# A gated mix of a Fourier layer and sliding-window attention: the order of the first loads, the start of a clearing, and three steps moved by a block or two

## The chip, the cores and the metric

One core of one Trainium2 chip. The metric is the device time of one execution in microseconds (us). The core has five engines that run side by side: TensorE (PE; its weight loads are PEld), VectorE (DVE), ScalarE (ACT), GpSimd (POOL) and SyncE (SP), which here issues nearly all transfers. 16 DMA engines carry them.

## The reference

x is 2048 rows of 512 (float32). The reference computes

```python
a, b = x @ dft_hid_re.T, x @ dft_hid_im.T
A = dft_seq_re @ a - dft_seq_im @ b
q, k, v = heads(x @ wqkv)              # 32 heads of 16
p = softmax(q k^T / 4, where 0 <= i - j < 256)
B = (p v, heads side by side) @ wo
g = sigmoid((x * gate_w).sum(-1))
out = g * A + (1 - g) * B
```

## The kernel before

**Products in two parts.** A float32 operand is split into a high part (a cast) and a low part (the value less the high part). A product is three matmuls, high x high, high x low and low x high, summed in PSUM (TERMS, L248). ScalarE, VectorE or GpSimd makes the high part; mostly VectorE makes the low one. `split` (L78) does both: its cast is L80 (ScalarE) or L82, its subtraction L85.

**The head (L147 to L164).** x comes transposed, in 4 slices of 128 input channels (dk) for each quarter `ss` of 512 rows. The first weights, `wqk[0]`, are 1024 columns: 256 (128 KB) for each dk. A slice of x for one `ss` is 128x512, 256 KB. ScalarE's queue issues two of the four slices of x (L155), SP's queue the other two and the four parts of the weights (`ld`, L55/L56). Then, for each dk in turn, ScalarE casts the weights (L162), x is split (for dk 0 both steps on VectorE, else the cast on ScalarE), and VectorE makes the weights' low part (L164). Inside this block the order of ScalarE, VectorE and SP is that of the code. TensorE first runs eight matmuls on zeros (`warm`, L593). `qk_first` (L263, matmuls L269) then makes the first quarter of q and k of head group 0: for each dk, three terms of two matmuls (q and k). `v_proj` (matmuls L304) follows; its weights `wv` are the next loads.

**Clearing (L198 to L219).** The tiles `pads` and `ring` hold q and k of one group in 96 of 128 partitions; 96 to 127 must be zero or hold the row maxima. GpSimd clears them: one `affine_select` into a pad (L203), whose condition never holds, so that every value is the fill 0, and which reads a part of the first x only to be ordered behind it; then eight memsets of 32x2048 (L200), each issued behind the last.

**Attention** runs over n = 4 groups x 32 blocks of 64 queries, 4 pairs of heads p in each. `s_pair` (L357) makes scores against 320 keys (L367); VectorE finds the row extreme (L369), ScalarE exponentiates and sums (L372). Every 8 blocks `ml_split`, `ml_turn` and `ml_rows` turn the extremes and the inverse sums and store them in DRAM (`m_scr`, `l_scr`). LAG = 19 blocks later `t_pair` (L436) makes the scores again, transposed, with keys on partitions, for block k = n - 19 (L449); ScalarE exponentiates (L450), GpSimd masks (L454, L458), and `pv` (L461, matmuls L475) multiplies by v for several blocks in one visit. When 8 blocks of a group are summed, `o_out` (L491) multiplies the sum by the inverse sums (L496) and stores it. `l_load` (L485) loads these inverse sums into one of five `ev` buffers, which also serve the partial results of the Fourier part.

**The Fourier part** is a generator, `dense` (L595). The loop (L1021) takes a few of its matmuls between the attention's (`fill`), so TensorE's order is written out by the code. The sequence products (L529) take pieces of `cr` and `ci`, 128x1024, loaded by SP into two `raw` buffers and split (L588); each piece feeds 24 matmuls. Partial sums go to DRAM (`r_scr`) and back.

**The output projection** (`wo_begin`, L911, matmuls L922) takes seven products for four blocks of a 2x2 split. What it needs first is made ahead of attention's end by the table BEFORE_END (L1007): `first_load` (attention outputs), `first_sums` (L876 to L879, sums on VectorE), `split_a(0)` and four `first_split`. A key (k, p) says after which block and pair a step is issued.

Outside the head a scheduler places the instructions of ScalarE, VectorE, GpSimd and SP; `behind` (L68) holds a step behind the last marked instruction of an engine.

Of the kernel before, what the change touches and what calls it, by code (L numbers as in the profile page):

```python
# [14 lines left out]
P = 128  # L15
S = 2048
D = 512
DK = D // P
NG = 4
NP = 4  # L20
# [12 lines left out]
def fnet_window_mix(ctx: ExitStack, tc: tile.TileContext, xT, x, wqk, wv, wr, wi, cr, ci, wo, gw, out):  # L33
    nc = tc.nc
# [20 lines left out]
    def ld(dst, src):  # L55
        mark("sp", nc.sync.dma_start(dst, src))  # L56

    def f(ap):
        return ap.bitcast(F32)
# [4 lines left out]
    def mark(e, ins):  # L64
        last[e] = ins.ins

    @contextmanager
    def behind(*engines):  # L68
        with ExitStack() as es:
            for e in engines:  # L70
                if e in last:
                    es.enter_context(tc.issue_after(last[e]))
            yield
# [4 lines left out]
    def split(hi, lo, raw, act=False):  # L78
        if act:
            nc.scalar.copy(hi, raw)  # L80
        else:
            cast = (nc.gpsimd if act is None else nc.vector).tensor_copy(hi, raw)  # L82
            if act is None:
                mark("pool", cast)
        return nc.vector.tensor_sub(lo, raw, f(hi))  # L85
# [43 lines left out]
    XT = {}  # L129
    XRAW = {}  # L130
# [7 lines left out]
    def split_x(ss, dks, act=False):  # L138
        for dk in dks:
            XT[dk, ss] = big.tile([P, 2, 512], F32R, name="big")  # L140
            mark("dve", split(XT[dk, ss][:, 0], XT[dk, ss][:, 1], XRAW.pop((dk, ss)), act))


    def pt_raw():
        return at.tile([P, NP, WIN], F32, name="pt", bufs=4).rearrange("p a b -> p (a b)")[:, :1024]

    with tc.manual_schedule(engines={mybir.EngineType.Activation, mybir.EngineType.DVE, mybir.EngineType.SP}):  # L147
        wraw, *xraw = [pt_raw() for _ in range(3)]
        wq0 = [st.tile([P, 1024], F32R, name=h) for h in ("hi", "lo")]
        zero = ev.tile([P, 512], F32R, name="ev")  # L150
        nc.vector.memset(f(zero[:]), 0.0)
        for dk in (0, 2, 1, 3):
            XRAW[dk, 0] = xraw[dk // 2][:, HALVES[dk % 2]]
            if dk % 2 == 0:
                nc.scalar.dma_start(XRAW[dk, 0], xT[0, dk])  # L155
        for dk in range(DK):
            ld(wraw[:, dk * 256:dk * 256 + 256], wqk[0][:, dk * 256:dk * 256 + 256])
            if dk % 2 == 0:
                ld(XRAW[dk + 1, 0], xT[0, dk + 1])
        for dk in range(DK):  # L160
            c = slice(dk * 256, dk * 256 + 256)
            mark("act", nc.scalar.copy(wq0[0][:, c], wraw[:, c]))  # L162
            split_x(0, (dk,), dk > 0)
            mark("dve", nc.vector.tensor_sub(wq0[1][:, c], wraw[:, c], f(wq0[0][:, c])))  # L164
# [3 lines left out]
    pads = [[const.tile([P, NP, P], F32R, name=f"pad{i}_{b}") for b in range(NPAD)] for i in range(2)]  # L168
# [4 lines left out]
    for h in (0, 64):  # L173
        m = mask[h:h + 64, :]
# [23 lines left out]
    def clear_rows(i, ss):  # L198
        with behind("pool"):
            mark("pool", nc.gpsimd.memset(f(ring[i][96:128, :, ss * 512:(ss + 1) * 512]), 0.0))  # L200

    first_hi = f(XT[0, 0][96:128, 0]).rearrange("r (p c) -> r p c", p=NP)
    mark("pool", nc.gpsimd.affine_select(pads[0][0][96:128], first_hi, pattern=[[0, NP], [0, P]],  # L203
                                         compare_op=OP.is_gt, fill=0.0, base=0, channel_multiplier=0))
    for ss in range(4):
        for i in (1, 0):
# [219 lines left out]
    def v_spread(n):  # L426
        if n >= NG * NB:
            return
        raw = VR.pop(n)
        v2 = vpad[n // 4 % 2]  # L430
        for h in range(2):
            nc.gpsimd.tensor_scalar(v2[:, :, :, 16 * h:16 * h + 16], raw.rearrange("r j (p d) -> r j p d", d=16),  # L432
                                    side[:, h:h + 1], None, op0=OP.mult)
        V2[n // 4] = v2
# [358 lines left out]
    def spots(i, n, c0):  # L793
        if c0 + 512 > S:
            return flat(i)[:, c0:c0 + n * S].rearrange("r (p s) -> r p s", s=S)[:, :, :512]
        return ring[i][:, :n, c0:c0 + 512]
# [3 lines left out]
    def os_spot(m, b):  # L800
        if m < 3:
            return spot(0, m, COL[b])
        if b and m == 6:
            return spot(0, 3, COL[0])
        return spot(1, m - 3, COL[b])

    def halves(t):
        return (t[:, :256], t[:, 256:]) if len(t.shape) == 2 else (t[:, :, :256], t[:, :, 256:])
# [7 lines left out]
    def wo_fetch(c):  # L816
        RAW[c] = [const.tile([P, 512], F32, name="tw", tag=f"pad0_{j}") for j in range(2)]
        for j in range(2):
            ld(RAW[c][j], wo[j][:, HALVES[c]])
# [4 lines left out]
    def wo_diffs(c):  # L824
        b11, b12, b21, b22 = (q for t in RAW[c] for q in quarters(t, 2))
        t1, t3, t2, t4 = spare()
        for t, x, y in ((t1, b12, b11), (t3, b22, b12), (t2, b22, t1), (t4, b21, t2)):
            nc.vector.tensor_sub(t, x, y)
        DIFF[c] = b11, b21, b22, t4, t1, t2, t3

    def fin_split(c, m):
        split(fin(m, 0, c), fin(m, 1, c), DIFF[c][m])
# [60 lines left out]
    def split_a(i):  # L893
        a, b = O[i][1]
        split(*halves(spots(0, 2, COL[i % 2])), a.rearrange("p (m t) -> p m t", m=2), True)
        split(*halves(os_spot(2, i % 2)), b[:, 256:], True)

    def first_split(m):
        split(*halves(os_spot(m, 0)), EX[0][m - 3], True)
# [69 lines left out]
    def ring_ahead(n):  # L969
        nonlocal loaded  # L970
        while loaded < 16:
            g, ss = divmod(loaded, 4)
            if n >= 32 * g + 8 * ss:
                need(("qk", g, ss))
            if ("qk", g, ss) not in have or n - LAG < 32 * (g - 1) + 8 * ss + 9:
                break
            with behind(*(("sp",) if g == 0 else ())):
                ring_load(g, ss)
            loaded += 1
# [10 lines left out]
    N = NG * NB  # L990
# [9 lines left out]
    def v_next(n):  # L1000
        if n < N:
            for c in range(2):
                need(("v", n % NB // 2 + c))
            with behind(*(("sp",) if n < 8 else ())):
                v_load(n)

    BEFORE_END = {(121, 3): first_load, (123, 0): first_sums, (123, 2): lambda: split_a(0)}  # L1007
    for c, k in enumerate((113, 118)):
        BEFORE_END[(110, 116)[c], 2] = lambda c=c: wo_fetch(c)
        BEFORE_END[k - 1, 1 + 2 * c] = lambda c=c: wo_diffs(c)  # L1010
        for j, m in enumerate((0, 1, 2, 4, 6, 5, 3)):
            BEFORE_END[k + j // 2, j % 2 * 2] = lambda c=c, m=m: fin_split(c, m)
    for j, m in enumerate((3, 5, 4, 6)):
        BEFORE_END[124 + j // 2, j % 2 * 2] = lambda m=m: first_split(m)

    def ahead_of_end(k, p):
        if (k, p) in BEFORE_END:
            with behind("pad1", "sp"):
                BEFORE_END[k, p]()

    for n in range(N + LAG + 1):  # L1021
        k = n - LAG
        if k == 0:
            masks.append(n)
        ring_ahead(n + 1)
        if k in (-1, 4):
            v_spread(0 if k < 0 else 4)
        if k in (-4, -1, 4):
            v_next({-4: 0, -1: 4, 4: 8}[k])
        if n == 0:  # L1030
            make_pad(0, 0)
        for p in range(NP):
            if n < N:
                s_pair(n, p)
            fill(n)
            visit = p == 0 and (k - summed >= (6 if more else 4) or k == N)
            if 0 <= k < N and not visit:
                t_pair(k, p)
            if p == 0:
                make_pad(0, n + 1)  # L1040
                if k >= -1:
                    make_pad(1, k + 1)
            fill(n)
            if visit:
                for j in range(summed, k):
                    pv(j)
                summed = k
                if k < N:
                    t_pair(k, p)
            ahead_of_end(k, p)  # L1050
            for at_n, at_p, do in TURN if n > 12 else FIRST:
                u, j = divmod(n - at_n, 8)
                if p == at_p and j == 0 and 0 <= u < 16:
                    do(u)
            if p == 3 and k % 8 == 6 and 0 <= k < N:
                l_load(k // 8)
            if p == 0 and full:
                o_out()
            if p == 3 and 4 * spread - 5 < summed and 4 * spread < N and n >= fresh:
                v_spread(4 * spread)  # L1060
                spread += 1
                v_next(4 * spread)
                fresh = n + 2
# [49 lines left out]
```

## Time and profile before

| | |
|---|---|
| median of three timed runs | 848.02 us (846.18 to 848.15) |
| the profiled execution: its own time | 846.26 us |
| its span, first to last instruction | 844.4 us |
| TensorE busy | 839.5 us, 5310 matmuls |
| VectorE / ScalarE / GpSimd busy | 644.3 / 609.0 / 295.0 us |
| DMA | 161.03 MB, mean 191 GB/s |

A row of the timeline gives the start, the time (of a run of like instructions, their count behind x), engine, line, operation, out<-in, and in brackets the idle time of the engine before it and what ended it. Rows of the waits give who waited for whom, the sum in us, how often, and the longest. Rows of the windows give each engine's busy time in a stretch, then PEclk, the DMA engines' share and GB/s. Recorded matmuls overlap, so their pace is read from start to start.

### The profile page before, as it was taken

Reading aid. Unit: us, or ns where it says so; the run is one execution under the profiler, and the core shown is the slowest. Engines: PE = TensorE matmul, PEld = TensorE weight load, DVE = VectorE, ACT = ScalarE, POOL = GpSimd, SP = SyncE. Lnnn points to the kernel's source line nnn. Section 1 sums busy time; section 2 is a strip of 40 time slices with the busy share of each in tenths; the row PEclk is TensorE's granted clock in tenths of the full one; section 3 lists DMA queues with packets and bytes.
Section 4 is the critical chain, followed back from the end, with each engine's and each line's share of the span. In section 5 each row is a group of like instructions: output and inputs, shape, how many; then the busy total and the mean of one; then the engine's idle time right before and its main releaser. Section 6 shows DMA issues by size and latency. Waiting matters only on the chain.

```text
span 844.4 us, 17173 instructions
## 1 busy us (share of the span) xinstructions
PE 839.5 (99%) x5310; PEld 695.9 (82%) x5310; DVE 644.3 (76%) x2083; ACT 609.0 (72%) x1832; POOL 295.0 (35%) x606
## 2 busy tenths in 40 slices
PE   9999999999999999999999999999999999999998
PEld 6888888888888788888888887878887878878997
DVE  5588978667878787787877877878987867666974
ACT  6488888878888897787977977867777865553330
POOL 8102332233232233242333243243232357746410
PEclk9999999999999999999999999999999999999999
DMA  8776678576765275544445557969873446546632
GB/s 300 246 226 182 219 244 253 189 236 224 211 230 173 69 209 123 179 124 121 140 138 148 166 156 216 299 207 315 276 218 120 137 141 199 169 157 233 210 133 92
DMA packets 94635, 161.03 MB, mean 191 GB/s; under 512 B 26832, under 2 KB 35792, under 8 KB 94544
## 3 DMA queue, kind: packets, MB, share of 16 engines
q1 hardware_dynamic: 94112, 159.28, 60.5%
q8 instruction: 42, 0.69, 0.4%
q10 hardware_dynamic: 432, 0.66, 0.2%
q14 instruction: 49, 0.40, 0.1%
HBM read 108.27 MB, written 51.64 MB: 189 GB/s over the span
## 4 chain that ended last, share of the span: by engine, by line
PE 99%; DVE 1%; issue 0%; ACT 0%; DVEq 0%; ACTq 0%
PE dc L529 42%; PE dab L304 10%; PE dqk L281 10%; PE t L449 9%; PE s L367 8%; PE o L475 8%; PE dv L304 5%; PE t L922 5%; PE s L269 1%; PE dv L593 0%; PE s L387 0%; DVE pad L350 0%; PE t L559 0%; DVE sm L369 0%; ACT sm L372 0%
## 5 line engine op out<-in xcount | busy, mean ns | idle before, releaser
L529 PE MATMUL dc<-big,hi 128*128 128x512 f32 x1020 | 344.6, 393 | 0.0
L372 ACT ACTIVATE sm<-sm,ml 128x320 f32<-128x320 f32 (+4 forms) x512 | 277.2, 542 | 59.4 <-DVE ml L369 54.1
L369 DVE CUSTOM_DVE_ANT_0 sm<-s,mask 128x320 f32<-128x320 f32 (+4 forms) x512 | 235.1, 464 | 107.9 <-PE s L367 74.6
L450 ACT ACTIVATE pt<-t 128x320 f32<-128x320 f32 (+4 forms) x392 | 159.1, 411 | 83.1 <-PE t L449 77.4
L529 PE MATMUL dc<-big,lo 128*128 128x512 f32 x510 | 200.2, 393 | 0.0
L529 PEld LDWEIGHTS dc<-big,hi 128*128 128x128 f32 x1020 | 179.4, 188 | 21.4
L454 POOL TENSOR_SCALAR_AFFINE_SELECT pt<-pt 128x128 f32<-128x128 f32 x196 | 73.9, 377 | 277.1 <-ACT pt L450 276.0
L449 PE MATMUL t<-ring,pad 128*128 128x320 f32 (+4 forms) x512 | 156.7, 306 | 0.0
L367 PE MATMUL s<-ring,pad 128*128 128x320 f32 (+4 forms) x512 | 155.1, 303 | 0.1
L350 DVE TENSOR_SCALAR pad<-ring,half 96x256 fp32r<-96x256 f32 x384 | 119.7, 358 | 4.0 <-PE t L449 3.6
L449 PEld LDWEIGHTS t<-ring,pad 128*128 128x128 f32 x512 | 96.1, 188 | 30.6 <-issue 8.7
L367 PEld LDWEIGHTS s<-ring,pad 128*128 128x128 f32 x512 | 96.1, 188 | 21.4 <-DVE ml L369 1.8
L529 PEld LDWEIGHTS dc<-big,lo 128*128 128x128 f32 x510 | 95.9, 188 | 12.0
L372 ACT ACTIVATION_READ_ACCUMULATOR sm<-sm,ml 128x1 f32 x512 | 97.4, 190 | 0.0
L588 DVE TENSOR_TENSOR lo<-raw,hi 128x512 fp32r<-128x512 f32 x137 | 94.8, 700 | 2.8 <-ACT hi L588 2.0
L304 PE MATMUL dab<-hi,big 128*128 128x512 f32 x256 | 88.9, 394 | 0.0
L281 PE MATMUL dqk<-big,hi 128*128 128x512 f32 x240 | 85.0, 393 | 0.0
L432 POOL TENSOR_SCALAR vpad<-vr,half 128x256 f32<-128x256 f32 x64 | 61.9, 979 | 65.1 <-PE o L475 29.5
L348 ACT ACTIVATE pad<-ring,half 96x256 fp32r<-96x256 f32 x128 | 66.8, 522 | 0.0
L588 DVE CAST hi<-raw 128x512 fp32r<-128x512 f32 x126 | 54.5, 439 | 13.3 <-PE dc L529 11.4
L454 POOL TENSOR_SCALAR_AFFINE_SELECT home<-home 128x128 f32<-128x128 f32 x60 | 32.6, 544 | 89.6 <-ACT home L450 86.6
L458 POOL TENSOR_SCALAR_AFFINE_SELECT pt<-pt 128x128 f32<-128x128 f32 x172 | 63.2, 368 | 0.0
(122 smaller groups left out, 1035.8 us busy)
## 6 DMA issues: line engine op xcount, KB each, us to landing
qk_scr<-home SPq DMA_DIRECT2D x32, 512.0 KB
ring<-qk_scr SPq DMA_DIRECT2D x32, 512.0 KB
raw<-cr SPq DMA_DIRECT2D x32, 512.0 KB
raw<-ci SPq DMA_DIRECT2D x32, 512.0 KB
r_scr<-ev SPq DMA_DIRECT2D x42, 256.0 KB
ab_scr<-home SPq DMA_DIRECT2D x20, 512.0 KB
big<-ab_scr SPq DMA_DIRECT2D x20, 512.0 KB
ring<-qk_scr SPq DMA_DIRECT2D x32, 256.0 KB
```

The source lines that it names most:

```text
L281: nc.tensor.matmul(ps, w[a][:, c:c + 128], XT[dk, ss][:, b], start=n == 0, stop=n == 11)
L304: nc.tensor.matmul(ps, XT[dk, ss][:, a, c * 128:(c + 1) * 128], wh[b], start=n == 0, stop=n == 11)
L350: mark(f"pad{i}", nc.vector.tensor_scalar(dst, src, half[:96, h:h + 1], None, op0=OP.mult))
L367: nc.tensor.matmul(ps[:, :w], PAD[0, n][:, p], ring[1][:, p, k0:k0 + w], start=True, stop=True)
L369: mark("dve", nc.vector.tensor_tensor_reduce(out=sm[:, :w], in0=ps[:, :w], in1=mask[:, WIN - w:], scale=1.0, scalar=3e38, op0=OP.add, op1= ...
L372: mark("act", nc.scalar.activation(sm[:, :w], sm[:, :w], AF.Exp, bias=nm[:, c], scale=-1.0, accum_out=l[:, c]))
L449: nc.tensor.matmul(ps[:, :w], PAD[1, n][:, p], ring[0][:, p, q0:q0 + w], start=True, stop=True)
L450: nc.scalar.activation(pt[:, p, :w], ps[:, :w], AF.Exp, scale=-1.0)
L454: nc.gpsimd.affine_select(a, a, pattern=[[0, 2], [2, 64]], compare_op=OP.is_ge, fill=0.0, base=1, channel_multiplier=-1)
L475: nc.tensor.matmul(OT[g, sb][32 * p:32 * p + 32, q - sb * 512:e - sb * 512], v2[:, p], pt[:, p, q - q0:e - q0], start=first, stop=kb == 8 ...
L529: nc.tensor.matmul(ps, w[a][:, i % 8 * 128:i % 8 * 128 + 128], ab[SC[i]][:, b], start=i == ends[0] and a + b == 0, stop=i == ends[1] and a ...
L588: return fn(*args)
```

## The change

Three edits. **First loads**: ScalarE's queue takes x's slices 0 and 1 (it had 0 and 2). SP's queue has the weights' parts 0 and 1, then x's slices 2 and 3 in one transfer of 512 KB, then the weights' parts 2 and 3 in one of 256 KB. It had part 0, slice 1, parts 1 and 2, slice 3, part 3. Two transfers fewer are issued, and `wv`'s two loads no longer wait for an earlier transfer's semaphore. **Clearing**: the select at L203 reads the low part of the first weights (repeated over p) in place of the high part of the first x, so GpSimd's clearing starts when that low part is made. **Moves**: `first_sums`, `split_a(0)` and the four `first_split` are issued one block later; `l_load` is issued at k % 8 == 5, p == 1, in place of k % 8 == 6, p == 3.

The order of instructions: TensorE's is unchanged; GpSimd's too, but for the select's operand. SP's has the new first loads, each load of inverse sums some transfers earlier, and some loads of partial results earlier or later, as `ev` buffers come free. VectorE's and ScalarE's differ near the end alone, where the moved steps come behind a block's pads.

```diff
-        for dk in (0, 2, 1, 3):
+        for dk in range(DK):
             XRAW[dk, 0] = xraw[dk // 2][:, HALVES[dk % 2]]
-            if dk % 2 == 0:
+            if dk < 2:
                 nc.scalar.dma_start(XRAW[dk, 0], xT[0, dk])
-        for dk in range(DK):
-            ld(wraw[:, dk * 256:dk * 256 + 256], wqk[0][:, dk * 256:dk * 256 + 256])
-            if dk % 2 == 0:
-                ld(XRAW[dk + 1, 0], xT[0, dk + 1])
+        for c in (slice(0, 256), slice(256, 512)):
+            ld(wraw[:, c], wqk[0][:, c])
+        ld(xraw[1].rearrange("p (k s) -> p k s", k=2), xT[0, 2:4].rearrange("k p s -> p k s"))
+        ld(wraw[:, 512:], wqk[0][:, 512:])
...
-    first_hi = f(XT[0, 0][96:128, 0]).rearrange("r (p c) -> r p c", p=NP)
-    mark("pool", nc.gpsimd.affine_select(pads[0][0][96:128], first_hi, pattern=[[0, NP], [0, P]],
+    first_lo = f(wq0[1][96:128, 0:P]).unsqueeze(1).to_broadcast([32, NP, P])
+    mark("pool", nc.gpsimd.affine_select(pads[0][0][96:128], first_lo, pattern=[[0, NP], [0, P]],
                                          compare_op=OP.is_gt, fill=0.0, base=0, channel_multiplier=0))
...
-    BEFORE_END = {(121, 3): first_load, (123, 0): first_sums, (123, 2): lambda: split_a(0)}
+    BEFORE_END = {(121, 3): first_load, (124, 0): first_sums, (124, 2): lambda: split_a(0)}
...
-        BEFORE_END[124 + j // 2, j % 2 * 2] = lambda m=m: first_split(m)
+        BEFORE_END[125 + j // 2, j % 2 * 2] = lambda m=m: first_split(m)
...
-            if p == 3 and k % 8 == 6 and 0 <= k < N:
+            if p == 1 and k % 8 == 5 and 0 <= k < N:
                 l_load(k // 8)
```

## The prediction

> **What bounds the kernel now.** I read the page first, then the timeline of the first 12 us, TensorE's waits in it, the waits of the whole run, and the chain. The profiled execution took 846.26 us for a span of 844.4, so 1.9 lie outside the span; it stands 1.8 under the median of the three timed runs (848.02; lowest 846.18, highest 848.15).
>
> ```profile
> span 844.4 us, 17173 instructions
> PE 839.5 (99%) x5310; PEld 695.9 (82%) x5310; DVE 644.3 (76%) x2083; ACT 609.0 (72%) x1832; POOL 295.0 (35%) x606
> PE 99%; DVE 1%; issue 0%; ACT 0%; DVEq 0%; ACTq 0%
> ```
>
> TensorE is on the chain nearly throughout. The change takes no matmul away, and the order of instructions shows TensorE's unchanged. It can win only where TensorE waits: at the head, and where a late load holds VectorE long enough to reach TensorE. The head, from the timeline (start, duration, engine, line, and idle time with what ended it):
>
> ```profile
> 1.51 3.50 PE L593 MATMUL dv<-ev 128*128 128x512 f32 x8 [1.51 <-DVE ev L151]
> 4.13 0.40 ACT L162 CAST hi<-pt 128x256 fp32r<-128x256 f32 x1 [1.13 <-DMA pt<-wqk]
> 4.32 0.43 DVE L82 CAST big<-pt 128x512 fp32r<-128x512 f32 x1 [1.14 <-DMA pt<-xT]
> 4.78 0.69 DVE L85 TENSOR_TENSOR big<-pt,big 128x512 fp32r<-128x512 f32 x1
> 4.88 1.09 POOL L203 TENSOR_SCALAR_AFFINE_SELECT pad<-big 32x512 fp32r<-32x512 f32 x1 [1.29 <-DVE big L82]
> 4.89 1.37 PE L269 MATMUL s<-big,hi 128*128 128x512 f32 x4
> 5.39 0.86 DVE L164 TENSOR_TENSOR lo<-pt,hi 128x256 fp32r<-128x256 f32 x1
> 5.92 14.10 POOL L200 MEMSET ring<- 32x2048 f32 x8
> 6.04 0.40 ACT L162 CAST hi<-pt 128x256 fp32r<-128x256 f32 x1 [1.51 <-DMA pt<-wqk]
> 6.30 0.30 PEld L269 LDWEIGHTS s<-big,lo 128*128 128x128 f32 x2 [0.48 <-DVE lo L164]
> 6.35 0.61 ACT L80 CAST big<-pt 128x512 fp32r<-128x512 f32 x1
> 7.00 0.69 DVE L85 TENSOR_TENSOR big<-pt,big 128x512 fp32r<-128x512 f32 x1 [0.75 <-ACT big L80]
> 7.61 0.42 DVE L164 TENSOR_TENSOR lo<-pt,hi 128x256 fp32r<-128x256 f32 x1
> 7.70 0.40 ACT L162 CAST hi<-pt 128x256 fp32r<-128x256 f32 x1
> 7.74 0.30 PEld L269 LDWEIGHTS s<-big,hi 128*128 128x128 f32 x2 [0.43 <-DVE big L85]
> 8.31 0.62 PE L269 MATMUL s<-big,lo 128*128 128x512 f32 x2
> 8.77 1.07 PE L269 MATMUL s<-big,hi 128*128 128x512 f32 x4
> 10.14 1.07 PE L269 MATMUL s<-big,hi 128*128 128x512 f32 x4
> 11.50 0.39 PE L304 MATMUL dv<-hi,big 128*128 128x512 f32 x1
> ...
> 33.48 0.19 PE L367 MATMUL s<-ring,pad 128*128 128x64 f32 x1
> ```
>
> From 8.77 to 10.14 six matmuls pass unhindered: 0.228 each. The 24 of `qk_first` run from 4.89 to 11.50, 6.61 where 24 x 0.228 = 5.47: **1.14 us is all that the head can give** unless the first matmul starts earlier. All of it lies in the first two slices of x (dk 0 and 1).
>
> **The change, part by part.** *First loads.* Call the quarters of the weights w0 to w3 and of x x0 to x3. w0 and x0 stay first in their queues, so the casts at 4.13 and 4.32 and the start at 4.89 stay. w1 now stands right behind w0, and x1 takes x2's place behind x0. x2 and x3 follow in one transfer, and w2 and w3 come last. What passed when:
>
> ```profile
> 0.00:2.00 2.00, 0.49 (x1) 0.49 (x2) 0.48 (x1) 0.29 (x1) 1.30 (x8) 1.00 0.06 7
> 2.00:4.00 2.00, 2.00 (x6) 1.52 (x6) 0.47 (x4) 0.99 (x1) 1.46 (x4) 1.00 0.85 255
> 4.00:5.00 1.00, 1.00 (x5) 0.61 (x4) 0.65 (x2) 0.40 (x1) 0.12 (x1) 1.00 1.03 395
> 5.00:6.00 1.00, 1.00 (x5) 0.46 (x4) 1.00 (x2) 0.00 (x0) 1.00 (x2) 1.00 1.06 383
> 6.00:7.00 1.00, 0.96 (x4) 0.30 (x2) 0.25 (x2) 0.96 (x3) 1.00 (x1) 1.00 1.10 410
> ```
>
> The last two columns are the DMA engines' share and GB/s: full from 4 us on, so the order of the loads decides, not their number. Summed, 14 KB had passed at 2.0, 524 at 4.0, 919 at 5.0, 1302 at 6.0. In before, w1 is complete with w0, x0, x1 and x2 before it (1049 KB, at 5.34), and its cast, which had waited for it, starts at 6.04: 0.70 after the bytes. I take 0.70 and allow 0.15 more, for later transfers pass in the same sums.
> After: w0, x0, w1 and x1 are 786 KB, at 4.66; visible near 5.4. ScalarE casts w1 at 5.4 and x1 0.31 later (as 6.04 to 6.35), to 6.33: 0.6 earlier than before. But w2 and w3 end the 1573 KB, at 6.66, and are visible at 7.36 to 7.5. In before w2 was cast right after x1, near 6.9, and x2 behind it. In after w2's cast starts at 7.4, x2's at 7.7 to 8.33, because ScalarE's order is w2, x2, w3, x3.
>
> *Clearing behind the first low part.* w0's low part took 0.86 where the same operation takes 0.42 at 7.61; the only other thing beside it is GpSimd's select (4.88 to 5.97). The select now waits for that low part, which so ends at 5.81: TensorE goes on at 5.86 in place of 6.30. The select then runs from 5.9 (1.09 at most: to 7.0, and half that if it too had been held up) and meets x1's low part.
> The Trainium skill ("GPSIMD Engine Reference", the specification table ahead of § 1.1) says that GpSimd's SBUF interfaces are shared with VectorE, with contention when a VectorE instruction has two SBUF inputs. The 0.86 agrees. By that rule the collision only moves on: x1's low part, also with two inputs, would end 0.44 later, and slice 2 would begin 0.2 later than in the sum below.
> The eight clearing memsets behind it start about a microsecond later; VectorE's 0.42 at 7.61, beside them, shows that they hold nothing up, and the first block's matmul needs them only at 33.48.
>
> *The head's sum.* Slice 1: TensorE is through slice 0 at 5.86 + 0.57 (a pair after a wait: 7.74 to 8.31) = 6.43, and x1's high part is there at 6.38. x1's low part ends at 6.35 + 0.69 = 7.04, so its pair starts at 7.1 in place of 7.74. Slice 1 ends 0.57 + 0.46 later, at 8.12 (8.77 before). Slice 2: x2's high part is there only at 8.38, 0.26 late. Its low part (8.36 + 0.69 = 9.05) lets the next pair go at 9.1, 0.15 late. Slice 3 begins at 9.1 + 0.57 + 0.46 = 10.13, where before has 10.14. **The head gains about 0.0**: 0.6 won on slice 1 is given back waiting for x2 and w2. Bounds: -0.65 if slice 2 does not wait at all; +0.6 if w2 and w3 are held up by as much as 256 KB at 410 GB/s. I take 0.0, for slice 2's gate hangs on the total of the bytes, which is the same.
>
> *Inverse sums.* They are loaded in the sixth block of each eight at p 1, where it was the seventh at p 3. What it cost:
>
> ```profile
> DVE ev L496 <- DMA ev<-l_scr: 4.8, 3, 2.1
> 139.43 0.64 SPq L56 DMA_DIRECT2D ev<-l_scr x1
> 143.95 0.69 DVE L496 TENSOR_TENSOR ev<-o,ev 128x512 f32<-128x512 f32 x1 [2.14 <-DMA ev<-l_scr]
> 143.07 0.31 PE L367 MATMUL s<-ring,pad 128*128 128x320 f32 x1
> 146.18 0.41 PE L449 MATMUL t<-ring,pad 128*128 128x320 f32 x1
> 118.51 2.29 PE o L475 x32
> 140.58 2.31 PE o L475 x64
> ```
>
> VectorE waited three times, 2.1 at the longest; TensorE felt it once that I can find, at 146.18, where one matmul shows 0.41 for 0.31. I count that twice, for the matmul behind it: 0.2 us. Two visits to `pv` are four blocks and 22 us apart, so 1.5 blocks are 8 us, and every one of these waits goes. I take -0.2 (0 to -0.5). On SP's queue the first moved load passes ten transfers (a, x, ring, row maxima and sums). It waits for nothing but one of the five `ev` buffers; its sums were stored blocks before. A buffer is held 8 us longer, and in exchange some loads of partial results (row blocks 7, 9 and 11) go later by several transfers; in the new order each still stands a few transfers ahead of the store that follows its add.
>
> *The end, one block later.* `first_sums`, `split_a` and `first_split` feed the first product of the output projection:
>
> ```profile
> 741.76 0.41 DVE L876 TENSOR_TENSOR sm<-oraw 128x256 f32<-128x256 f32 x1
> 748.10 0.41 DVE L85 TENSOR_TENSOR ring<-mask,ring 128x256 fp32r<-128x256 f32 x1
> 766.13 2.87 PE t L922 x24
> ```
>
> Now they end near 752; TensorE's other matmuls cover that until 766. Cost 0; without that cover, a block, 3 to 5 us. On the way the pads come ahead of the sums in VectorE's order, which can only help TensorE. I allow 0.3 either way for waits near the end.
>
> **Sum**: 0.0 - 0.2 + 0 = -0.2: 846.06 against 846.26 of the profiled execution, or 847.8 against the median. Runs of before fall on two levels, near 846.2 and near 848.1; I forecast for the median, **847.8**.
>
> **Rivals.** (1) *The two queues do better*: w2 lands early enough that slice 2 goes on at 8.12, the head gives its 0.65 and the loads 0.5. Then 848.02 - 1.15 = 846.9. For: ScalarE idled 1.51 for w1. Against: the same bytes come ahead of w3. (2) *The head loses*: wv's first half is issued behind w3 without a wait, and if the engines serve it together with w2 and w3, these land up to 0.64 late, slice 2 at 9.0: with the loads 848.4. It decides once the quarters are visible after 7.5. (3) *SP is blocked*: a moved load finds no `ev` buffer free and holds SP and the pieces of cr and ci queued behind it. The row for it:
>
> ```profile
> SPq L56 <- DVE lo L588: 126.7, 44, 19.6
> ```
>
> SP already stands up to 19.6 us at a time for buffers, so it has time to give. A piece feeds 24 matmuls, 5.5 us with none between; one that comes later than that stops TensorE for the rest: 3 us more in one place gives 850.8, slower. Against: by the trace the buffers are free when SP comes. (4) *TensorE's clock*: the eight warm-up matmuls took 3.50, 0.43 each, against 0.228 later: half rate until about 4.6 us. Were the change of rate later in the runs of after, each early matmul costs 0.2 more; by the spread of before's own runs up to 2.0, so 848.0 to 849.8.
> The Trainium skill ("TensorE: Matmul & The Clock Gate", Part 1) says that the window which decides this runs free of the kernel's start, so that the count of slow matmuls varies by run. The spread of before agrees but doesn't show the cause.
> (5) *It does not do what it says*: the loads move and TensorE never felt them: 848.0.
>
> **How the numbers follow.** Forecast 0.55, with (5) inside it; (1) 0.20; (2) 0.12; (3) 0.05; (4) 0.08. 0.3% is 2.5 us, about what a measurement can tell here. Faster by that needs (1) and the lower level in after: 0.07. Slower: (3) and a little of (4), 0.06. Within: 0.87. The range takes in (1), (2) and both levels: 845.3 (846.26 - 1.0) to 849.0.
>
> **What would show it.** Right: the cast of x1 near 5.7 and of x2 near 7.7, a new wait of TensorE's loads for ScalarE ahead of slice 2, the first L304 at 11.5, w0's low part at 0.42, and no wait of L496 on `l_scr`. Wrong: a first L304 at 10.9 (1) or past 11.8 (2), a TensorE wait for `hi` or `lo` of L588 (3), more than eight matmuls 0.43 apart (4).

## The result, and the profile after

| | before | changed |
|---|---|---|
| median of 22 runs each | 847.66 us | 845.53 us |
| lowest, highest | 846.18, 850.19 | 844.86, 846.66 |
| the profiled execution: own time, span | 846.26, 844.4 | 845.10, 843.3 |

The ratio is 0.9972, with an interval of 0.9965 to 0.9978: 2.1 us less, where the forecast was 0.2 less. The time lies inside the range, but by luck: the low end, 845.3, was set by a head that gains (rival 1) and by the lower of two supposed levels, and the gain came from neither. Not only the median fell: before's runs spread over 4.0 us, the changed kernel's over 1.8. The two profiled executions lie 1.2 us apart, and each is one draw from its spread; before's was nearly its fastest run.

The page of the changed kernel: span, busy times and chain.

```profile
span 843.3 us, 17171 instructions
PE 838.5 (99%) x5310; PEld 695.8 (83%) x5310; DVE 643.8 (76%) x2083; ACT 611.1 (72%) x1832; POOL 298.8 (35%) x606
PE 99%; DVE 1%; issue 0%; ACT 0%; DVEq 0%; ACTq 0%
```

TensorE has as many matmuls and is busy 1.0 us less; it still bounds the kernel. Its head, from the timeline (the same steps that the prediction quotes of before):

```profile
4.92 0.41 ACT L162 CAST hi<-pt 128x256 fp32r<-128x256 f32 x1 [0.48 <-DMA pt<-wqk]
5.05 1.21 PE L269 MATMUL s<-big,hi 128*128 128x512 f32 x4
5.34 0.62 ACT L80 CAST big<-pt 128x512 fp32r<-128x512 f32 x1
5.38 0.42 DVE L164 TENSOR_TENSOR lo<-pt,hi 128x256 fp32r<-128x256 f32 x1
5.94 0.64 POOL L203 TENSOR_SCALAR_AFFINE_SELECT pad<-lo 32x512 fp32r<-32x512 f32 x1 [2.34 <-DVE lo L164]
6.00 1.11 DVE L85 TENSOR_TENSOR big<-pt,big 128x512 fp32r<-128x512 f32 x1 [0.20 <-ACT big L80]
6.09 0.62 PE L269 MATMUL s<-big,lo 128*128 128x512 f32 x2
6.52 8.83 POOL L200 MEMSET ring<- 32x2048 f32 x5
7.04 0.41 DVE L164 TENSOR_TENSOR lo<-pt,hi 128x256 fp32r<-128x256 f32 x1
7.17 0.30 PEld L269 LDWEIGHTS s<-big,hi 128*128 128x128 f32 x2 [0.42 <-DVE big L85]
7.35 0.41 ACT L162 CAST hi<-pt 128x256 fp32r<-128x256 f32 x1 [1.39 <-DMA pt<-wqk]
8.33 0.30 PEld L269 LDWEIGHTS s<-big,hi 128*128 128x128 f32 x2 [0.41 <-ACT big L80]
11.46 0.39 PE L304 MATMUL dv<-hi,big 128*128 128x512 f32 x1
```

The head's time is the one forecast: w1 and x1 come earlier (4.92 and 5.34), w0's low part takes 0.42 again, x1's low part meets the select instead (1.11 where 0.69 is usual), and slice 2 waits at 8.33 for w2 and x2. The first L304 stands at 11.46, against 11.50: nothing gained. In the twenty profiles (these two and those of the runs below) it stands anywhere from 11.39 to 12.45, so one pair of profiles says little; e1 and e2 below measure it.

The waits of the changed kernel for L496 and for pieces of ci, and VectorE's timeline at two of the multiplications:

```profile
DVE ev L496 <- PE o L475: 23.2, 15, 3.2
DVE hi L588 <- DMA raw<-ci: 0.7, 1, 0.7
```

```profile
142.26 0.69 DVE L496 TENSOR_TENSOR ev<-o,ev 128x512 f32<-128x512 f32 x1 [0.76 <-PE o L475]
...
272.51 0.24 DVE L245 RECIPROCAL g<-ge 128x16 f32<-128x16 f32 x1
272.67 0.63 DVE L496 TENSOR_TENSOR ev<-o,ev 128x512 f32<-128x512 f32 x1
```

The waits of L496 for `l_scr` are gone, as forecast. But one more went that the forecast had not counted. In before, VectorE's timeline at the same place reads:

```profile
272.97 0.24 DVE L245 RECIPROCAL g<-ge 128x16 f32<-128x16 f32 x1
274.26 0.69 DVE L496 TENSOR_TENSOR ev<-o,ev 128x512 f32<-128x512 f32 x1 [1.05 <-PE dab L304]
```

The idle 1.05 us there is put down to a matmul of another tile (`dab`), which L496 doesn't read: the name of a neighbour that happened to end, not of the cause. It is the fourth load of inverse sums that was late (in e5 below the row of the same stand names it), and in the changed kernel the idle time at this place is nil. Which of the edits gives the 2.1 us, and by what way, the runs below decide.

### The profile page after: what moved, and what is told of

Its sections match the earlier page's. It is cut to its first block, busy times and chain, and to the rows that moved or that the text cites. A ratio compares the mean times of both kernels' runs of the same rounds, so it can differ in the third digit from the quotient of the medians.

```text
span 843.3 us, 17171 instructions
## 1 busy us (share of the span) xinstructions
PE 838.5 (99%) x5310; PEld 695.8 (83%) x5310; DVE 643.8 (76%) x2083; ACT 611.1 (72%) x1832; POOL 298.8 (35%) x606
## 4 chain that ended last, share of the span: by engine, by line
PE 99%; DVE 1%; issue 0%; ACT 0%; DVEq 0%; ACTq 0%
PE dc L529 42%; PE dab L304 11%; PE dqk L281 10%; PE t L449 9%; PE s L367 8%; PE o L475 8%; PE dv L304 5%; PE t L922 5%; PE s L269 1%; PE dv L593 0%; PE s L387 0%; DVE pad L350 0%; PE t L559 0%; DVE sm L369 0%; ACT sm L372 0%
## 5 line engine op out<-in xcount | busy, mean ns | idle before, releaser
L529 PE MATMUL dc<-big,hi 128*128 128x512 f32 x1020 | 344.7, 393 | 0.0
L369 DVE CUSTOM_DVE_ANT_0 sm<-s,mask 128x320 f32<-128x320 f32 (+4 forms) x512 | 235.5, 465 | 111.4 <-PE s L367 71.2
L529 PE MATMUL dc<-big,lo 128*128 128x512 f32 x510 | 200.2, 393 | 0.0
L529 PEld LDWEIGHTS dc<-big,hi 128*128 128x128 f32 x1020 | 179.3, 188 | 21.4
L454 POOL TENSOR_SCALAR_AFFINE_SELECT pt<-pt 128x128 f32<-128x128 f32 x196 | 77.1, 393 | 275.0 <-ACT pt L450 273.7
L350 DVE TENSOR_SCALAR pad<-ring,half 96x256 fp32r<-96x256 f32 x384 | 120.0, 359 | 5.4 <-PE t L449 4.9
L529 PEld LDWEIGHTS dc<-big,lo 128*128 128x128 f32 x510 | 95.9, 188 | 12.0
L304 PE MATMUL dab<-hi,big 128*128 128x512 f32 x256 | 88.9, 394 | 0.0
L458 POOL TENSOR_SCALAR_AFFINE_SELECT pt<-pt 128x128 f32<-128x128 f32 x172 | 62.9, 366 | 0.0
```

Source lines behind the costliest of these rows:

```text
L304: nc.tensor.matmul(ps, XT[dk, ss][:, a, c * 128:(c + 1) * 128], wh[b], start=n == 0, stop=n == 11)
L350: mark(f"pad{i}", nc.vector.tensor_scalar(dst, src, half[:96, h:h + 1], None, op0=OP.mult))
L369: mark("dve", nc.vector.tensor_tensor_reduce(out=sm[:, :w], in0=ps[:, :w], in1=mask[:, WIN - w:], scale=1.0, scalar=3e38, op0=OP.add, op1= ...
L454: nc.gpsimd.affine_select(a, a, pattern=[[0, 2], [2, 64]], compare_op=OP.is_ge, fill=0.0, base=1, channel_multiplier=-1)
L529: nc.tensor.matmul(ps, w[a][:, i % 8 * 128:i % 8 * 128 + 128], ab[SC[i]][:, b], start=i == ends[0] and a + b == 0, stop=i == ends[1] and a ...
```

## The experiments

Each kernel was timed against before on the same chip; before's medians in the five groups were 847.83, 848.07, 847.82, 847.90 and 847.91 (e, e5 on, f and h, g, k). "Moved" means l_load at k % 8 == 5, p == 1, as in the change.

| kernel | what | median | ratio to before |
|---|---|---|---|
| e1 | first loads alone | 847.62 | 1.0001 (0.9987 to 1.0016) |
| e2 | clearing alone | 848.51 | 1.0009 (1.0000 to 1.0018) |
| e3 | all inverse sums moved, alone | 845.79 | 0.9977 (0.9967 to 0.9986) |
| e4 | end alone | 848.33 | 1.0003 (0.9992 to 1.0014) |
| e5 | the change without the sums | 847.92 | 1.0003 (0.9994 to 1.0012) |
| e6 | before, L496 two pairs later | 846.13 | 0.9981 (0.9972 to 0.9990) |
| e7 | sums half a block ahead in code | 846.02 | 0.9977 (0.9967 to 0.9986) |
| e8 | sums half a block later in code | 847.35 | 0.9996 (0.9987 to 1.0004) |
| f1 | fourth load alone moved | 847.05 | 0.9989 (0.9980 to 0.9998) |
| f2 | first three moved | 848.30 | 0.9999 (0.9988 to 1.0010) |
| f3 | fifth to last moved | 846.88 | 0.9992 (0.9983 to 1.0001) |
| g1 | tenth alone | 847.45 | 0.9992 (0.9983 to 1.0000) |
| g2 | fourth and tenth | 846.34 | 0.9979 (0.9971 to 0.9988) |
| g3 | e3, fifth to last loaded again in the old place | 847.83 | 0.9997 (0.9986 to 1.0008) |
| k1 | fourth, fifth, tenth | 846.48 | 0.9984 (0.9975 to 0.9993) |
| k2 | all but these three | 846.99 | 0.9989 (0.9980 to 0.9999) |
| h1 | the change, other head | 845.91 | 0.9974 (0.9964 to 0.9985) |
| g4 | the change, L496 two pairs later | 845.51 | 0.9966 (0.9953 to 0.9978) |

### Which edit

e1 is the first hunk of the change alone, e2 the second (L203), e4 the two of BEFORE_END, and e3 this one:

```diff
-            if p == 3 and k % 8 == 6 and 0 <= k < N:
+            if p == 1 and k % 8 == 5 and 0 <= k < N:
                 l_load(k // 8)
```

> The kernel before with the first loads alone changed. Its runs spread over 4.0 us (846.2 to 850.2, median 847.7), the changed kernel's over 1.8 (844.9 to 846.7, median 845.5); the two profiled runs differ by 1.06 us of span only. Theory A (late inverse sums make VectorE and TensorE wait by amounts that vary from run to run, and the moved loads end that): here no change, 847.3 to 848.0, spread near 4 us, first L304 at 11.5 +-0.3. Theory B (the head varies from run to run, by its loads or by the clock, and the new loads steady it): 845.8 to 846.5, spread near 2 us. Theory C (the end): as A here. Theory D (many small waits, each edit its part): 847.0 to 847.6.

> The kernel before with the clearing alone moved behind the first low part. Theory A and C: no change, 847.3 to 848.0. In the profile the first low part of the weights takes 0.42 us where it took 0.86, TensorE goes on after slice 0 0.3 to 0.45 earlier, but then waits for slice 1's high part, so the first L304 stands within 0.1 of 11.50. Theory B: 846.0 to 847.0, if the collision with GpSimd is what varied. Theory D: 847.3 to 847.7.

> The kernel before with the loads of the inverse sums alone moved 1.5 blocks ahead. Theory A: 845.5 to 846.3 and a spread near 2 us; no wait of L496 on the loads. Theory B and C: 847.2 to 847.7 (0.0 to 0.5 us, what the profile of before shows of such waits), spread near 4 us. Theory D: 846.8 to 847.4.

> The kernel before with the steps ahead of the output projection alone moved by one block. Theory C (TensorE waits in the last 60 us by amounts that vary, and the moved steps end that): 845.8 to 846.8. Theories A and B: no change, 847.3 to 848.0. Theory D: 847.2 to 847.6; the profile of the changed kernel shows 0.2 to 0.3 us less of waits past 740 us.

e3 has all of the gain (845.79), and its narrow spread (844.95 to 846.74); the other three have none of it. Two of the rows expected of the head did not come: the first L304 stands at 12.45 in e1 (11.5 +-0.3) and at 12.01 in e2 (within 0.1 of 11.50), where already the first loads came late and the first matmul of `qk_first` started at 5.36. e5 is the changed kernel with the edit of e3 undone:

```diff
-            if p == 1 and k % 8 == 5 and 0 <= k < N:
+            if p == 3 and k % 8 == 6 and 0 <= k < N:
```

> The changed kernel with the loads of the inverse sums put back where they were (first loads, clearing and end as changed). The moved loads alone gave 845.8 against 847.8 of before, the other three edits alone 847.6, 848.5 and 848.3. Theory A (late inverse sums hold VectorE and through it TensorE): the whole gain is lost, 847.4 to 848.6, spread 3 us or more. Theory D (many small waits, edits that help one another): 846.3 to 847.2.

847.92, spread 3.1: theory A. The inverse sums are the whole change in time; no other edit gains anything measurable, and e2's interval, 1.0000 to 1.0018 around 0.7 us more, just reaches 1. e1's profile shows one danger of the first loads: w2 and w3 came late there.

```profile
8.33 0.40 ACT L162 CAST hi<-pt 128x256 fp32r<-128x256 f32 x1 [1.95 <-DMA pt<-wqk]
...
9.30 0.73 PE L269 MATMUL s<-big,hi 128*128 128x512 f32 x2 [0.81 <-ACT big L80]
```

Slice 2 begins at 9.30, 0.97 later than in the changed kernel with the same loads. That is what the prediction's rival (2) describes, in one run; that `wv` held up w2 and w3 is not shown.

### VectorE's stand at L496

The stand itself, in e5 (VectorE, then TensorE):

```profile
274.86 0.69 DVE L496 TENSOR_TENSOR ev<-o,ev 128x512 f32<-128x512 f32 x1 [1.74 <-DMA ev<-l_scr]
275.47 0.48 DVE L369 CUSTOM_DVE_ANT_0 sm<-s,mask 128x320 f32<-128x320 f32 x1
```

```profile
274.94 0.39 PE L304 MATMUL dab<-hi,big 128*128 128x512 f32 x1
276.01 0.41 PE L367 MATMUL s<-ring,pad 128*128 128x320 f32 x1 [0.69 <-DVE ml L369]
```

Here the releaser is named rightly. VectorE idles 1.74 us, the row extremes (L369) behind L496 come late, and TensorE's next score matmul with them: 1.07 us from start to start where 0.23 is usual, 0.84 lost. To tell the stand (A1) from the transfer itself (A2), e6 leaves the loads and moves the multiplication; e7 and e8 change the lead of the loads.

```diff
 e6
-            if p == 0 and full:
+            if p == (2 if k < N else 0) and full:
 e7
-            if p == 3 and k % 8 == 6 and 0 <= k < N:
+            if p == 1 and k % 8 == 6 and 0 <= k < N:
 e8
-            if p == 3 and k % 8 == 6 and 0 <= k < N:
+            if p == 1 and k % 8 == 7 and 0 <= k < N:
```

> The kernel before, with the loads of the inverse sums where they were, but the multiplication by them (L496) issued two pairs later, some 2.7 us, except for the very last. Theory A1 (VectorE stands at L496 until the sums land, and what is queued behind it there comes late): the same cure from the other end, 845.6 to 846.6, no idle time of VectorE ahead of L496 beyond 0.3 us near 144, 187, 230 and 275. Theory A2 (the transfer itself, 256 KB at that place of SP's queue, holds up the transfers behind it, and L496's wait is only a sign): no gain, 847.4 to 848.3.

> The kernel before with the loads of the inverse sums half a block (about 2.7 us) ahead in place of 1.5 blocks. VectorE's wait at L496 was 1.2 to 1.9 us longer than in the kernel with the loads moved by 1.5 blocks, so under theory A1 half a block is nearly enough: 845.7 to 846.6. Theory A2 (place in SP's queue): anything, near 847.5 if only the old neighbourhood counts. If the wait is longer in unprofiled runs than in the profiled ones, between: 846.6 to 847.2.

> The kernel before with the loads of the inverse sums half a block later. Theory A1: VectorE stands 2.7 us longer at each of the four multiplications that follow their load closely (near 144, 187, 230, 275), 3.5 to 5 us each, which TensorE's lead does not cover: 0.5 to 2 us each, so 850 to 856. Theory A2 and D: within 1 us of before, 847 to 849.

e6 and e7 came out as A1 has it (846.13, 846.02). e6's waits show what it did: L496 stands for TensorE's products 5.4 us in all, where before had 19.9, and for no load.

```profile
DVE ev L496 <- PE o L475: 5.4, 3, 2.8
```

e8 missed: 847.35 instead of 850 or more. The loads that count weren't later. SP issued its first at 135.58, before's at 139.43, and the second, third and fourth within 0.3 us of before's (the second at 181.23 there); only some of the later ones, the sixth and the ninth for instance, came 3 us later.

```profile
135.58 0.66 SPq L56 DMA_DIRECT2D ev<-l_scr  x1
180.96 0.64 SPq L56 DMA_DIRECT2D ev<-l_scr  x1
```

The place in the code isn't the place in SP's queue, which the scheduler sets. So e8 decides nothing between A1 and A2. The same holds for e7: half a block in the code put the tenth load at 514.53, where 1.5 blocks put it at 514.76 and before at 525.62.

### Which loads

The condition picks the loads u = k // 8 that are moved; f1: u == 3, f2: u < 3, f3: u > 3, g1: u == 9, g2: u in (3, 9), k1: u in (3, 4, 9), k2: u not in (3, 4, 9).

```diff
-            if p == 3 and k % 8 == 6 and 0 <= k < N:
+            if 0 <= k < N and (p, k % 8) == ((1, 5) if k // 8 == 3 else (3, 6)):
                 l_load(k // 8)
```

> The kernel before with one load of inverse sums moved 1.5 blocks ahead, the fourth (its multiplication near 275). The kernels with the late load show TensorE stopped there by 0.2, 0.25, 0.5, 0.95 and 0.95 us in five profiled runs. Theory A1, counted at this place alone: 847.1 to 847.5 (0.6 us less than 847.8 to 848.1 of before). If what follows (a stop of 0.25 to 1.4 near 541 in three of those five runs, none in three of the four with the wait cured) hangs on it as well: 846.2 to 846.9. If it is the other places that matter: 847.7 to 848.2.

> The kernel before with the first three loads of inverse sums moved 1.5 blocks ahead (multiplications near 144, 187 and 230). TensorE's stops there are 0.0 to 0.2 us in the profiled runs. Theory A1 counted by the profile: 847.6 to 848.0. If these waits cost more in unprofiled runs than in the profiled ones: 846.4 to 847.3.

> The kernel before with the loads of inverse sums from the fifth on moved 1.5 blocks ahead. There the multiplication waits for TensorE's products in every profile, not for the load. Theory A1: no gain, 847.5 to 848.2. Theory A2 (the transfer of the tenth load, issued near 527, holds up the piece of cr that VectorE waits for near 541, where TensorE stops by 0.25 to 1.4 in three of five profiles): 846.6 to 847.4.

f1 gave 0.8 us less, f2 nothing, f3 0.9 less. f1 is the stand at 275. f2 fits too: VectorE stands some 2 us at the first two of its places, and TensorE hardly feels it (the prediction's row at 146.18). f3 contradicts A1, for from the fifth load on L496 waits for TensorE's products in before and in f3, never for the load. (The last multiplication is an exception in two other kernels: f1's row at 763.57 reads 3.34 <-PE dc L529, a matmul of another tile once more, and f1 and g2 start it 1.25 and 1.02 us after the start of its last product, where it is 0.36 in before, f3 and the changed kernel.) Its interval just reaches 1, so f3 alone is weak; but the rows of VectorE's waits for pieces of cr speak with it. In e5, f1 and f3 they are (f3 has none for cr):

```profile
DVE hi L588 <- DMA raw<-cr: 1.8, 1, 1.8
```

```profile
DVE hi L588 <- DMA raw<-cr: 1.4, 1, 1.4
```

```profile
DVE hi L588 <- DMA raw<-ci: 1.3, 1, 1.3
```

Of the ten profiled kernels with the later loads in the old place (before, e1, e2, e4, e5, e6, e8, f1, f2, and g3 below), nine wait for a piece of cr, near 322 or 541, 0.3 to 4.1 us in all; only e6 does not. Of the six with all of them moved (the changed kernel, e3, e7, f3, h1, g4), one does. The fifth load was issued near 311 and the tenth near 526, each ten us or more ahead of such a place. What moving does to the queue, from the windows of f1 (first) and e3:

```profile
522.00:526.00 4.00, 4.00 (x23) 3.37 (x23) 3.57 (x13) 2.99 (x11) 1.07 (x5) 1.00 0.61 164
526.00:530.00 4.00, 4.00 (x22) 3.42 (x21) 3.45 (x14) 3.15 (x13) 1.03 (x4) 1.00 0.98 306
...
534.00:538.00 4.00, 4.00 (x21) 3.48 (x20) 3.53 (x13) 3.37 (x12) 0.87 (x4) 1.00 1.07 198
```

```profile
522.00:526.00 4.00, 4.00 (x23) 3.38 (x22) 3.70 (x12) 3.05 (x11) 1.13 (x4) 1.00 1.02 286
526.00:530.00 4.00, 4.00 (x22) 3.43 (x21) 3.46 (x15) 3.28 (x13) 0.72 (x2) 1.00 1.02 372
...
534.00:538.00 4.00, 4.00 (x21) 3.47 (x20) 3.15 (x11) 3.58 (x11) 1.17 (x4) 1.00 1.01 324
```

In f1 (this profile is the longest of its runs) the DMA engines stand partly idle from 522 to 526 (share 0.61) and are full from then on; in e3, with the load issued at 514, they are full there as well. In f1 the engines are as full at 534 to 538 but move 198 GB/s against 324. The tenth load's 256 KB stand in the full stretch, ahead of the piece. That alone doesn't make the piece late: k2, with the tenth load at 526, shows nearly f1's figures (share 0.57, then 200 GB/s) and no wait for cr.

g1, g2, k1 and k2 divide further; g3 puts the transfer back without its wait, by loading the same sums a second time into the same tile (256 KB more for each):

```diff
 (e3, and behind it)
+            if p == 3 and k % 8 == 6 and 32 <= k < N:
+                ls = l_scr[k // 8]
+                with behind("sp"):
+                    ld(RL[k // 8], bass.AP(tensor=ls.tensor, offset=ls.offset, ap=[[512, 2 * NP], [0, 16], [1, 512]]))
```

> The kernel before with the tenth load of inverse sums alone moved 1.5 blocks ahead (issued near 514 in place of 526). VectorE waits for a piece of cr near 541 in every profiled kernel with the tenth load near 526 but one (0.3 to 2.8 us), in none with it near 514. Theory A2 (at 526 its 256 KB stand ahead of the piece in the transfers' queue): 846.9 to 847.3, the same as all loads from the fifth on moved (846.9), and no wait for the piece. If the later loads help in another way, or the fifth to ninth count too: 847.5 to 848.1.

> The kernel before with the fourth and the tenth load alone moved 1.5 blocks ahead. Theories A1 for the fourth and A2 for the tenth together: all of the gain, 845.7 to 846.4. If the other loads matter: 846.6 to 847.2.

> The kernel with all loads of inverse sums moved ahead (845.8), and the loads from the fifth on made a second time, into the same tile, where they stood before: 256 KB more each, in the old place. Nothing else waits for them that is late. Theory A2 (the transfer in the old place is what costs): the gain of the later loads is lost again, 846.5 to 847.2, and VectorE waits for a piece of cr near 541 as before. If an early load helps only because its own result is early: 845.6 to 846.2.

g3 gives all of e3's gain back (847.83), though the fourth load stays early, and its profile, one of its two longest runs (850.10), shows how. First SP's queue, then VectorE, then TensorE:

```profile
526.21 0.63 SPq L56 DMA_DIRECT2D ev<-l_scr  x1
...
532.06 0.53 SPq L56 DMA_DIRECT2D raw<-cr  x1
```

```profile
538.36 0.75 DVE L707 SCALAR_TENSOR_TENSOR ev<-dc,g,ev 128x512 f32<-128x512 f32 x1
542.47 0.43 DVE L588 CAST hi<-raw 128x512 fp32r<-128x512 f32 x1 [3.37 <-DMA raw<-cr]
542.81 0.87 DVE L350 TENSOR_SCALAR pad<-ring,half 96x256 fp32r<-96x256 f32 x3
```

```profile
541.46 0.39 PE L529 MATMUL dc<-big,lo 128*128 128x512 f32 x1
544.15 0.41 PE L449 MATMUL t<-ring,pad 128*128 128x320 f32 x1 [2.30 <-DVE ml L369]
```

VectorE stands 3.37 us at a cast of the piece, the pads and row extremes queued behind it are late, and TensorE stops: 2.69 from start to start, 0.23 usual. In e3 the same cast follows L707 without idle time:

```profile
538.73 0.74 DVE L707 SCALAR_TENSOR_TENSOR ev<-dc,g,ev 128x512 f32<-128x512 f32 x1
539.40 0.42 DVE L588 CAST hi<-raw 128x512 fp32r<-128x512 f32 x1
```

So transfers of this size in the old place can cost, without anybody waiting for them. (g3 also carries 12 x 256 KB more in all, so its price is that of added transfers, and more than that of moved ones.) g2 came out near the expected whole (846.34); g1 between its two expectations (847.45).

> The kernel before with three loads of inverse sums moved 1.5 blocks ahead: the fourth (VectorE stood for it near 275), the fifth (issued near 311, ahead of a piece of cr that VectorE waited for near 321 in four profiled kernels) and the tenth (526, piece of cr near 541). The fourth and tenth together gave 846.3. If these three places are all: 845.6 to 846.1. If the fifth counts for nothing: 846.2 to 846.6.

> The complement: all loads of inverse sums moved ahead but the fourth, fifth and tenth. If those three places are all: no gain, 847.4 to 848.3, with a wait for the fourth load near 275 and, in most profiles, for a piece of cr near 321 or 541. If the gain is spread over many loads: 846.5 to 847.2.

Both came out as in their second case. k1 gives 1.4 us of the 2.0, no more than g2, so the fifth load is not seen to count; k2 gives 0.9, so the three places are not all. In k2's profile the stand at the fourth load is there (L496 at 274.56 after 1.19 us idle), and no piece of cr is late although the fifth and tenth load stand in the old place.

Where TensorE itself falls behind can be read in all twenty profiles, for its 5310 matmuls have the same order in each: the time from the first start to the last start of a stretch, less that of the quickest profile. In us, lowest to highest (mean):

| stretch | the load | kernels with it in the old place | the others |
|---|---|---|---|
| 140 to 150 | first | 10: 0.01 to 0.36 (0.18) | 10, with e6 and e8: 0.00 |
| 272 to 278 | fourth | 10: 0.30 to 1.21 (0.70) | 10, with e6: 0.00 to 0.11 (0.03) |
| 318 to 334 | fifth | 12: 0.00 to 1.00 (0.14) | 7: 0.00 |
| 539 to 544 | tenth | 10: 0.00 to 1.41 (0.45) | 9: 0.00 to 1.15 (0.13) |
| 781 to 785 | later ones | 14: 0.14 to 0.69 (0.36) | 6: 0.00 to 0.04 (0.01) |

(g3, which has the transfer in both places, is left out at the fifth and the tenth. The 1.15 is g4's alone. In the last row the six have all or nearly all of the later loads moved by 1.5 blocks and none repeated: the changed kernel, e3, f3, h1, g4 and k2; e7 stands with the fourteen.) The five differences of the means add up to 1.7 us, near the 2.0 of e3, and the fourth load's 0.67 is near f1's 0.8. At the fourth load the two groups don't overlap, so the stand there is shown. The last row is a place that no expectation names. In f1 it reads:

```profile
782.41 1.75 PE L922 MATMUL t<-ring 128*128 128x256 f32 x12
784.43 0.98 PE L922 MATMUL t<-ring 128*128 128x256 f32 x6 [0.27 <-DVE rt L926]
```

TensorE stops for VectorE there. Since k1 has this stop (0.57) and k2 hasn't, it is part of what k1 lacks and k2 has. Why it comes is open: e7 has it too (0.53), though its last two loads stand where e3's do. The intervals of the single kernels, some 0.8 us to each side, allow no finer division.

### Versions to beat both

h1 orders the first loads by need with none in one transfer, and lets the select wait for the last low part of the weights. g4 is the changed kernel with e6's edit.

```diff
-        for c in (slice(0, 256), slice(256, 512)):
-            ld(wraw[:, c], wqk[0][:, c])
-        ld(xraw[1].rearrange("p (k s) -> p k s", k=2), xT[0, 2:4].rearrange("k p s -> p k s"))
-        ld(wraw[:, 512:], wqk[0][:, 512:])
+        for dk in range(DK):
+            ld(wraw[:, dk * 256:dk * 256 + 256], wqk[0][:, dk * 256:dk * 256 + 256])
+            if dk > 1:
+                ld(XRAW[dk, 0], xT[0, dk])
...
-    first_lo = f(wq0[1][96:128, 0:P]).unsqueeze(1).to_broadcast([32, NP, P])
+    first_lo = f(wq0[1][96:128, 768:896]).unsqueeze(1).to_broadcast([32, NP, P])
```

> The changed kernel with another order of the first loads: ScalarE's queue x0 and x1 as changed, SP's queue w0, w1, w2, x2, w3, x3, each on its own; and the select ahead of the clearing reads the last low part of the first weights in place of the first. In the changed kernel x1's low part took 1.11 us beside the select where 0.69 is usual, and slice 2 waited for w2 and x2, both visible past 7.3. Expected from the rows: slice 1's low pair at 6.8 (7.5 before it: 7.50 in the changed kernel), x2's cast at 6.4 to 6.8, slice 2 without a wait near 7.9, the first L304 at 10.5 to 10.9 (11.46): 0.6 to 0.9 us less, 844.6 to 845.0 against 845.5. If the time ahead of 12 us is taken back at the next loads (wv): the first L304 earlier, but the time 845.3 to 845.7. If clearing that ends near 25 us comes too late for the first block at 33: slower than 845.7.

> The changed kernel, and the multiplication by the inverse sums (L496) two pairs later on VectorE, except for the last. Either alone cures VectorE's stand at the loads (845.5 and 846.1), so by that theory nothing more comes: 845.3 to 846.0. In the changed kernel VectorE still stands 23 us at L496 for TensorE's products, 1.5 at a time; if what is queued behind it there reaches TensorE: 844.5 to 845.2.

Neither is measurably better than the changed kernel (845.91 and 845.51 against 845.53). h1 missed its 844.6 to 845.0. In h1 x2's cast came at 6.97 and TensorE waits for nothing in slices 1 to 3, and yet the first L304 stands at 11.62:

```profile
5.09 1.91 PE L269 MATMUL s<-big,hi 128*128 128x512 f32 x4
6.80 0.89 PE L269 MATMUL s<-big,lo 128*128 128x512 f32 x2
7.52 1.09 PE L269 MATMUL s<-big,hi 128*128 128x512 f32 x4
...
11.62 0.39 PE L304 MATMUL dv<-hi,big 128*128 128x512 f32 x1
```

The first six matmuls start 0.43 apart (5.09 to 6.80 for four), the half rate of the warm-up, up to 7.2; in the changed kernel four had passed from 5.05 to 6.09. In this run the half rate took what the loads gave. (PEclk in the rows of the windows reads 1.00 in these stretches of both kernels, so it doesn't show this half rate; the starts do.) Whether h1 wins in the mean could not be measured.

## Why the prediction was right, and where it failed

**The head: right.** 0.0 was forecast, 0.04 seen, and e1 and e2 measure no gain (e1's interval goes from 1.1 us less to 1.4 more). Slice 2 at 8.33 (forecast 8.38) and L304 at 11.46 held. Slice 1's low pair at 7.17 (forecast 7.1) is luck, two errors that cancel: w1 and x1 were cast 0.5 and 0.4 us ahead of the forecast (4.92 and 5.34 for 5.4 and 5.7), for the 0.70 us between bytes and cast was too long, and x1's low part then took 0.42 more than the sum has, beside the select. The rule that the collision with the select only moves on, cited there, is borne out by the 1.11 of x1's low part. The Trainium skill ("SBUF — State Buffer", "SBUF: two separate sides") says why the memsets do no harm: an instruction of VectorE with two SBUF inputs is shut out only by a GpSimd operation that reads SBUF. The select reads, and the memsets behind it did nothing to the 0.41 of the next low part; the trace agrees.

**The inverse sums: the failed step.** The term for the loads of inverse sums in the sum was a tenth of what it should have been: "I count that twice, for the matmul behind it: 0.2 us ... and every one of these waits goes. I take -0.2 (0 to -0.5)." Measured alone: -2.0 (0.9977, that is -1.2 to -2.8). For the one place that it counted, near 146, 0.2 was right: the ten kernels with that stand lose 0.18 there in the mean. Three things were missing from that sum:

1. The fourth wait of L496, at 274.26, was not in the row for `l_scr`, because its releaser was put down to a matmul. It is the costly one: TensorE stops there for 0.70 us in the mean of ten profiles, and f1, which moves this load alone, gains 0.8 us.
2. The step followed the moved load past ten transfers and asked only what it would do to those. It did not ask what its 256 KB had done where they stood. Put back there without a wait (g3) they cost the whole gain; from the fifth load on, moving gives 0.9 (f3). This part is less sure than the first: g3 has more transfers in all, and f3's interval just reaches 1.
3. The size was taken from one execution that was nearly before's fastest. In it the stand at 274 is 1.05 us long and VectorE waits 0.7 for cr; in e5 they are 1.74 and 1.8. The prediction read the three timed runs as "two levels, near 846.2 and near 848.1"; 22 runs fill the stretch from 846.2 to 850.2. The spread was the sign of the stops, and the change removes stops that come in most profiles.

**The end: right.** 0 was forecast; e4 shows 1.0003 (0.9992 to 1.0014).

**The rivals.** (1) asked for the head and the loads together; the loads alone went past its 0.5, the head did nothing. (2)'s late slice 2 was seen in one run of e1, not in the median. (3), SP blocked: TensorE shows no stop of 3 us in the changed kernel. (4), a later change of rate: seen in h1, and in kernels with the old head too (in e7 and k1 the first matmuls of `qk_first` are still 0.43 apart), so it doesn't take the change to bring it. (5), that TensorE never felt the loads, is refuted by e3 and e5.

**Open.** Why the loads from the fifth on count, above all near 783; and why e6, which leaves the transfers where they were, has nearly all of the gain as well. e6 also cuts L496's stand for TensorE's products (5.4 us, 19.9 before), but g4, which adds this to the change, gains nothing by it. One profile of e6 shows no wait for cr, and one of g4 shows 1.5 us with the tenth load early: the place may change how often the piece is late, and does not fix it.

## What to carry to other kernels

Price a load twice: by who waits for it, and by what stands behind it in the same queues; moving it out of a full stretch can help whoever comes next, even if its own result was never late. When the idle time ahead of an instruction is put down to something that it doesn't read, look for the operand that it does read and see when that landed. And look at the spread of the timed runs before taking a price from one profile: this kernel, whose runs spread over 4 us, had stops that one of its fastest runs hardly showed.

## What was not expected of the hardware

The DMA engines at a full share carried 198 GB/s in one stretch of f1 and 372 in another of e3: here a full share says nothing of the rate, and by these two rates 256 KB take an estimated 0.7 or 1.3 us.

TensorE's warm-up begins at 1.51 in each profile, and its rate doubles at about 4.5 us in before, at about 5 in the changed kernel and only past 7 in h1. The Trainium skill ("TensorE: Matmul & The Clock Gate", Part 1) has the point of change vary by some 0.5 us either way; these runs lie further apart.

VectorE's pads (L350) slow down beside GpSimd, though they have one tensor as input. In e2 two of them took 1.94 us while GpSimd ran a split; in e3, where GpSimd began later, two took 0.61:

```profile
85.64 1.94 DVE L350 TENSOR_SCALAR pad<-ring,half 96x256 fp32r<-96x256 f32 x2
```

```profile
85.53 0.61 POOL L588 CAST hi<-raw 128x512 fp32r<-128x512 f32 x1 [3.42 <-DMA raw<-wi]
86.10 2.63 POOL L588 TENSOR_TENSOR lo<-raw,hi 128x512 fp32r<-128x512 f32 x2
```

```profile
85.08 0.61 DVE L350 TENSOR_SCALAR pad<-ring,half 96x256 fp32r<-96x256 f32 x2
```

In e2 the split had waited 3.42 us for a load of `wi`. A transfer that lands at another time thus moves GpSimd's work beside other work of VectorE, and a run's time with it: from 84 to 88 us TensorE falls 0.5 behind in e2 and at most 0.1 in the other profiles. That such meetings make up part of the spread is argued, not shown.
